# One step's opening of a filter block split in two: seeds copied a step ahead, factors and first products ahead of the slots

## The chip, the cores and the metric

The kernel runs on one core of one Trainium2 chip. The metric is the device time of one execution in microseconds (us). Engines: PE (TensorE, matrix products), DVE (VectorE), ACT (ScalarE), POOL (GpSimd) and SP (SyncE, which issues the DMAs). [...]

## What is computed

Two independent heads over 2048 positions and 448 channels, side by side in the output. Head A is a long convolution (S4D): its filter K is a sum over 256 complex states per channel, applied by FFT. Head B is softmax attention with 16 heads of 28 channels.

```
def _A_ref(u, log_A_real, A_imag, C_real, C_imag, log_dt, D_skip):
    dt = exp(log_dt); A = -exp(log_A_real) + 1j * A_imag
    C = (C_real + 1j * C_imag) * dt[:, None]
    P = exp((A * dt[:, None])[:, :, None] * pos[None, None, :])
    K = 2.0 * einsum("dn,dnl->dl", C, P).real
    y = irfft(rfft(u_t, 2 * L) * rfft(K, 2 * L), 2 * L)[:, :, :L]
    return y.transpose(0, 2, 1) + u * D_skip
def _B_ref(x, wqkv, wo):
    q, k, v = split(x @ wqkv)               # 16 heads of 28
    p = softmax(q @ k.T * scale)
    return (p @ v) @ wo
return concatenate([a, b], axis=-1)
```

## The kernel before

The kernel has three parts in time. Up to about 260 us it projects q, k and v and makes the seeds of the filter (functions inside the first `with`). Then a loop of NS = 256 steps does the attention; into its gaps goes everything else of head A. A short tail ends it.

A step is one block of 128 keys for one block of 512 queries and four heads. Its order is written out by hand in `ORDER` (line 33), and every engine keeps the order of the program in this part (`KEPT["a"]`). The entries of `ORDER`:

- `m0` to `m3` (`max_mm`, line 166): one score product per head for the row maximum of a later step, written into a buffer `pm` of PSUM. `m0` (shown as `pm<-kdif,qhat`) is read by ACT (`rl`, Relu), `m1` by a custom DVE instruction that also reads `rl`, `m2` and `m3` by a DVE maximum (`mx<-pm`).
- `s0` to `s3` (`s_mm`, line 700): the scores of this step into one of three buffers `pss`; ACT makes the exponential `p` from each.
- `pv` (`pv_step`, line 707): the product of the previous step's `p` with v, `po<-p,v`.
- `f`: a slot (`slot`, line 936), a place for one other piece of work that uses PE. `slot` takes, in this order, urgent work (sums, scaling and maxima of a finished block of queries), output projections, the products of a filter block (`m_due`), the transform of u (`u_due`), and spectrum and finish jobs of the convolution. A slot with nothing due stays empty. Its product also goes to a buffer `pm`.
- `v` (`vec`, line 975): takes one operation from the queue of DVE work of the open filter block.
- `k`: closes a finished filter block (`k_next`, line 968), opens one where it is due (`k_begin`, line 951), and issues three of its POOL operations.

`pm` has three buffers taken in turn by `w_tile` (line 123), until the filter blocks are done; then a ring of four.

A filter block is the filter of eight channels; there are NB = 56, and block b is due at step 3.5 b. It has two tables, e (built on POOL by nine operations, `e_power`, line 620) and g (built on DVE by nine queue entries, `g_powers`, line 634). Both grow by doubling from seeds that a DMA has brought as `sdb` (three buffers, `load_sd`). g also needs the factors `zg`, a bank of PSUM of its own with one buffer. The first entry of g's queue, `lowest`, is three small operations on 128x128 elements; the others are one operation each (`first(1, 8)`, `second(1, 8)` and its addition on 128x256; `first(2, 16)` on 128x512; two halves of `second(2, 16)` and their additions on 128x256). With three `v` and three POOL operations a step, a block is built in three steps.

`k_start` (line 609) opens a block: it takes buffers for e, g and zg and makes three copies on ACT: the seeds of g, the factors zg, the seeds of e. It is called by `k_begin`, which then fills the queues and sets the products of the block due KD = 5 steps later: two tasks of 16 products on e and g (`k_mm`, `pm<-e,g`), evicted by ACT as `ko`, then one on `ko` (`pm<-w,ko`), evicted as `yk`. e and g have two buffers each, so a block's seeds overwrite those of the block before last; `done["mm"]` keeps which block's products are issued.

From step 192 on, spectrum jobs fill the slots (`spectrum`, line 762): two forward tasks (`pm<-yk,mw`, whose DVE products are `pr`, and `p` on DVE and POOL behind the second) and two backward ones (`pm<-p,mw`), and then finish jobs.

Of the kernel before, what the change touches and what calls it, by code (L numbers as in the profile page):

```python
# [7 lines left out]
F32 = mybir.dt.float32  # L8
F32R = mybir.dt.float32r
I32 = mybir.dt.int32  # L10
AF = mybir.ActivationFunctionType
# [12 lines left out]
CQ = 512  # L24
# [5 lines left out]
NU = G * NQ  # L30
NS = NU * NK
LEAD = 3
ORDER = ('m0', 's0', 'm1', 's1', 'v', 'f', 'pv', 'k', 'f', 'v', 'm2', 's2', 'm3', 's3', 'v')
PB = 8
F1 = 2
FX, PD, GAP = 1, 2, 2
# [5 lines left out]
K0, KP, KD, UP = 0, 3.5, 5, 3  # L42
# [14 lines left out]
SDF = F_Z + 18 * 16  # L57
Z_G = 9 * 16
# [30 lines left out]
def body(ctx, tc, a, out):  # L89
    nc = Engines(tc)  # L90
# [4 lines left out]
    def pool(stack, name, bufs=1, space=None, side=None):  # L95
        kw = {} if space is None else {"space": space}
        if side:
            kw["side"] = side
        return stack.enter_context(tc.tile_pool(name=name, bufs=bufs, reuse_waits="tile", **kw))
# [450 lines left out]
    ps_g = pool(ps_st, "ps_g", 1, PSUM)  # L550
# [52 lines left out]
    sds, egs = {}, {}  # L603

    def load_sd(b):
        sds[b] = g_p.tile([128, SDF], F32, name="sdb", bufs=3)
        nc.sync.dma_start(sds[b], sd_d[b // BO][b % BO])

    def k_start(b):
        sd = sds[b]  # L610
        e = g_p.tile([128, 2, 16, N2], F32, name="e", bufs=2)
        g = g_p.tile([128, 2, 16, N1], F32, name="g", bufs=2)
        zg = ps_g.tile([128, CQ], F32, name="zg")
        egs[b] = e, g
        zgs[b] = zg
        nc.scalar.activation(g[:, :, :, :4], sd[:, F_G:F_Z].rearrange("p (c h e) -> p c h e", c=2, e=4), AF.Copy)
        nc.scalar.activation(zg[:, :Z_G], sd[:, SDF - Z_G:], AF.Copy)
        nc.scalar.activation(e[:, :, :, :8], sd[:, :F_G].rearrange("p (c h e) -> p c h e", c=2, e=8), AF.Copy)

    def e_power(b, i, q):  # L620

        t, m = egs[b][0], 8 << i
        zz = sds[b][:, F_Z:].rearrange("p (k f h) -> p k f h", k=6, f=3)
        if q == 0:
            zr = zz[:, i, 0, :][:, None, :, None].to_broadcast([128, 2, 16, m])
            nc.gpsimd.tensor_tensor(t[:, :, :, m:2 * m], t[:, :, :, :m], zr, ALU.mult)
        elif q == 1:
            uts[0] = g_p.tile([128, 2, 16, 32], F32, name="eu")[:, :, :, :m]
            zi = zz[:, i, 1:3, :][:, :, :, None].to_broadcast([128, 2, 16, m])
            nc.gpsimd.tensor_tensor(uts[0], t[:, ::-1, :, :m], zi, ALU.mult)  # L630
        else:
            nc.gpsimd.tensor_tensor(t[:, :, :, m:2 * m], t[:, :, :, m:2 * m], uts[0], ALU.add)

    def g_powers(b):

        t, zg = egs[b][1], zgs[b]
        zz = zg[:, :Z_G].rearrange("p (k f h) -> p k f h", k=3, f=3)
        tt = nc.vector.tensor_tensor

        def first(i, m):  # L640
            tt(t[:, :, :, m:2 * m], t[:, :, :, :m], zz[:, i, 0, :][:, None, :, None].to_broadcast([128, 2, 16, m]), ALU.mult)

        def second(i, m, c):
            n = c.stop - c.start
            u = zg[:, CQ // 2:CQ // 2 + n * 16 * m].rearrange("p (c h m) -> p c h m", c=n, m=m)
            zi = zz[:, i, 1 + c.start:1 + c.stop, :][:, :, :, None].to_broadcast([128, n, 16, m])
            tt(u, t[:, ::-1, :, :m][:, c], zi, ALU.mult)
            return lambda: tt(t[:, c, :, m:2 * m], t[:, c, :, m:2 * m], u, ALU.add)
        both, u = slice(0, 2), {}

        def lowest():
            first(0, 4)
            second(0, 4, both)()
        ops = [lowest, lambda: first(1, 8), lambda: u.update(a=second(1, 8, both)), lambda: u["a"](), lambda: first(2, 16)]
        for c in (slice(0, 1), slice(1, 2)):
            ops += [lambda c=c: u.update(a=second(2, 16, c)), lambda: u["a"]()]
        return ops

    uts, zgs = {}, {}
# [56 lines left out]
    def load_og(u):  # L716
        og_u[u] = og = kq_p.tile([128, G - 1, CQ], F32, name="og")
        nc.sync.dma_start(og, on_d[u % NQ][:G - 1].rearrange("g p q -> p g q"))
# [138 lines left out]
    powers = {"g": collections.deque(), "e": collections.deque()}  # L857
    done = {"mm": -1}
# [19 lines left out]
    k_due = collections.deque(range(NB))  # L878
# [31 lines left out]
    def f_slot(s_, kind):  # L910
        f_load(s_, kind)
        if not f_tasks[kind]:
            if not f_loaded[kind] or f_loaded[kind][0][0] > s_:
                return False
            f_tasks[kind].extend(f_loaded[kind].popleft()[1])
            f_load(s_, kind)
        gap, t = f_tasks[kind][0]
        if n_slot[0] < f_next[kind] + gap:
            return False
        f_tasks[kind].popleft()  # L920
        t()
        s_done[0] += kind == "s" and not f_tasks[kind]
        f_next[kind] = n_slot[0]
        f_load(s_, kind)
        return True
# [10 lines left out]
    def slot(s_):  # L936
# [11 lines left out]
        else:  # L948
            f_slot(s_, "s") or f_slot(s_, "f")

    def k_begin(s_):
        if not (k_due and K0 + k_due[0] * KP <= s_ and done["mm"] >= k_due[0] - 2 and not powers["e"] and not powers["g"]):
            return
        b = k_due.popleft()
        k_start(b)
        powers["g"] += g_powers(b)
        powers["e"] += [lambda i=i, q=q: e_power(b, i, q) for i in range(3) for q in range(3)]
        p0, p1, p2 = k_mm(b)

        def m1():  # L960
            p1()
            done["mm"] = b
        m_due.extend((s_ + KD, t_) for t_ in (p0, m1, p2))
        last[0] = b
# [3 lines left out]
    def k_next():  # L968

        if last[0] is not None and not powers["e"] and not powers["g"]:  # L970
            if last[0] + 2 < NB:
                load_sd(last[0] + 2)
            last[0] = None

    def vec():
        if powers["g"]:
            powers["g"].popleft()()

    prev = None
    for s in range(NS):  # L980
        u, kt = divmod(s, NK)
        sm = s + NK + LEAD
        if s == 12 * NK:
            k0_st.close()
            f_p["s", 0] = f_p["s", 1] = pool(f0_st, "f0_p", side="right")
            f_ready["s", 0], f_ready["s", 1] = s, NS
        if s >= 12 * NK and f_ready["s", 1] == NS and not (k_due or m_due or powers["g"] or powers["e"]):
            g_st.close()
            ps_st.close()
            ps_w[:] = pool(ps_st, "ps_f", 4, PSUM), 1  # L990
            f_ready["s", 1] = s + F1
        if kt == 12 and u // NQ == G - 1:
            load_og(u)
        late[0] = s + NK + LEAD > NS
        if u % NQ == NQ - 1 and u < NU - 1 and kt % 4 == 2:
            load_v(u // NQ + 1, kt // 4)
        if sm < NS and sm // NK % NQ == NQ - 1 and sm % NK % 4 == 0 and sm % NK and sm // (NQ * NK) + 1 < G:
            load_kd(sm // (NQ * NK) + 1, sm % NK // 4 - 1)
        if sm < NS and sm % (NQ * NK) == 0 and sm:
            load_kd(sm // (NQ * NK), HG - 1)  # L1000
        if kt % 4 == 1 and u % NQ == 1 and u // NQ + 1 < G:
            load_k(u // NQ + 1, kt // 4, k_pools[(u // NQ + 1) % 2])
        if kt == 2:
            if u + 2 < NU:
                load_q(u + 2)
        ps = []
        for op in ORDER:
            if op[0] == "s":
                ps.append(s_mm(u, kt, int(op[1])))
            elif op[0] == "f":  # L1010
                slot(s)
            elif op[0] == "v":
                vec()
            elif op == "k":
                k_next()
                k_begin(s)
                for _ in range(3):
                    if powers["e"]:
                        powers["e"].popleft()()
            elif op == "pv":  # L1020
                if prev:
                    pv_step(*prev)
                    if prev[1] == NK - 1:
                        fin(prev[0], s)
            elif sm < NS:
                max_mm(sm // NK, sm % NK, int(op[1]))
        for _ in range(FX if late[0] else 0):
            slot(s)
        if sm < NS and sm % NK == NK - 1:
            def end(un=sm // NK):  # L1030
                max_end(un, w_tile())
                max_put(un)
            max_join(sm // NK)
            soon_slot(UG[0], end)
        k_next()
        prev = (u, kt, ps)
    pv_step(*prev)
    fin(prev[0], NS)
    s = NS
# [63 lines left out]
```

## Time and profile before

| | us |
|---|---|
| median of 3 runs | 1368.82 |
| lowest and highest | 1365.33, 1370.16 |
| the profiled execution's own time | 1366.65 |
| its span, first to last instruction | 1364.9 |
| PE busy in the span | 1243.5 |
| DVE busy | 980.3 |
| ACT busy | 968.6 |
| POOL busy | 831.0 |
| mean granted clock of TensorE | 0.975 of full speed |

All instructions of the loop show line 73, that of a helper, so groups are told apart by the names of what they write and read: `g<-g,zg` is an operation on table g, `e<-e,eu` one on e, `mx<-pm` a row maximum, `po<-p,v` PV. In a timeline the columns are start, duration (of the merged row), engine, line, operation, written and read tiles with shapes, count, and in brackets the idle time of the engine before it with what ended it. Rows of matrix products overlap: the modelled end of one lies behind the start of the next, so their spacing is read from the starts. In a list of waits the columns are the total, the number and the longest.

### The profile page before, as it was taken

To read this page: it belongs to the slowest core of one execution; us is meant where nothing else is said; L and a number is where in the kernel's file an instruction comes from. 1 tells how busy PE (TensorE), PEld (TensorE's weight loads), DVE (VectorE), ACT (ScalarE), POOL (GpSimd) and SP (SyncE) were. 2 spreads that over 40 slices of the span, in tenths; PEclk is the share of its full clock that TensorE was granted. 3 is DMA by queue.
4 is the path that set the end of the run, shared out by engine and by line. 5 is a ranking of instruction groups with operands and counts; after the bars stand their busy time and mean duration, and the time that the engine had idled before them with its cause. 6 is when DMAs were issued, how large, how long until landed. Compare 5 with 4: busy or idle time off the path is not lost.

```text
span 1364.9 us, 33230 instructions
## 1 busy us (share of the span) xinstructions
PE 1243.5 (91%) x12625; PEld 707.2 (52%) x12625; DVE 980.3 (72%) x2138; ACT 968.6 (71%) x2069; POOL 831.0 (61%) x705
## 2 busy tenths in 40 slices
PE   6978784799999999999999999999998999998997
PEld 4866662355555555555555555555555545544433
DVE  5778765877777777777788888887887766857311
ACT  4867662488888888888888888878786665655553
POOL 3576661187877877878878988888896111202221
PEclk9988896999999999999999999999999999999999
DMA  6775679726675546378533233632324544636476
GB/s 194 241 243 193 219 263 246 208 62 140 160 168 119 131 125 155 109 205 209 161 96 88 64 72 78 148 86 66 77 66 139 181 123 154 208 109 205 138 192 178
DMA packets 200729, 205.37 MB, mean 150 GB/s; under 512 B 96632, under 2 KB 159160, under 8 KB 198520
## 3 DMA queue, kind: packets, MB, share of 16 engines
q1 hardware_dynamic: 200568, 203.23, 53.5%
q8 instruction: 100, 1.64, 0.5%
q14 instruction: 61, 0.50, 0.1%
HBM read 120.73 MB, written 82.18 MB: 149 GB/s over the span
## 4 chain that ended last, share of the span: by engine, by line
PE 58%; DVE 16%; ACT 11%; POOL 5%; DMA 5%; issue 3%; SPq 0%; ACTq 0%; DVEq 0%; POOLq 0%
PE pm L73 34%; PE po L73 13%; PE pss L73 12%; ACT p L73 6%; DVE mx L73 3%; POOL qhat L73 3%; DVE g L73 2%; ACT rl L73 2%; DVE p L73 2%; DMA khat<-k 2%; DVE tri L73 1%; DVE pr L73 1%; DVE px L73 1%; POOL x_e L73 1%; DVE sg L73 1%
## 5 line engine op out<-in xcount | busy, mean ns | idle before, releaser
L73 ACT ACTIVATE p<-pss 128x512 f32<-128x512 f32 x1024 | 565.3, 608 | 137.0 <-PE pss L73 128.4
L73 PE MATMUL pss<-qhat,khat 128*128 128x512 f32 x1024 | 402.2, 399 | 3.5 <-ACT p L73 3.4
L73 DVE TENSOR_REDUCE mx<-pm 128x1 f32<-128x512 f32 x500 | 321.4, 683 | 104.6 <-PE pm L73 103.4
L73 PE MATMUL pm<-khat,qhat 128*128 128x512 f32 x749 | 329.7, 443 | 41.5 <-DVE mx L73 36.1
L73 POOL TENSOR_TENSOR e<-e,sdb 128x256 f32<-128x256 f32 x168 | 201.9, 1202 | 166.0 <-ACT e L73 157.0
L73 PE MATMUL po<-p,v 128*32 128x512 f32 x2048 | 271.8, 598 | 0.0
L73 POOL TENSOR_TENSOR e<-e,eu 128x256 f32<-128x256 f32 x168 | 248.5, 1479 | 13.2
L73 PEld LDWEIGHTS pm<-khat,qhat 128*128 128x128 f32 x749 | 141.0, 189 | 217.7 <-DVE mx L73 83.4
L73 PEld LDWEIGHTS pss<-qhat,khat 128*128 128x128 f32 x1024 | 190.6, 188 | 45.9 <-issue 11.1
L73 DVE CUSTOM_DVE_ANT_0 rl<-pm,rl 128x512 f32<-128x512 f32 x249 | 171.5, 689 | 47.3 <-ACT rl L73 44.2
L73 POOL TENSOR_TENSOR eu<-e,sdb 128x256 f32<-128x256 f32 x168 | 201.8, 1201 | 0.0
L73 DVE TENSOR_TENSOR g<-g,zg 128x128 f32<-128x128 f32 x392 | 162.9, 416 | 46.6 <-ACT zg L73 41.5
L73 ACT ACTIVATE rl<-pm 128x512 f32<-128x512 f32 x249 | 150.8, 606 | 24.9 <-PE pm L73 24.9
L73 POOL TENSOR_TENSOR p<-pr,pr 64x448 f32<-64x448 f32 x32 | 40.9, 1277 | 191.7 <-DVE pr L73 180.6
L73 PE MATMUL pm<-kdif,qhat 128*128 128x512 f32 x249 | 100.9, 405 | 2.4 <-DMA v<-v 1.3
L73 PEld LDWEIGHTS pm<-e,g 128*32 128x32 f32 x3584 | 63.0, 110 | 52.8 <-issue 30.9
L73 DVE TENSOR_TENSOR zg<-g,zg 128x128 f32<-128x128 f32 x224 | 87.5, 391 | 1.9
L73 PEld LDWEIGHTS po<-p,v 128*32 128x32 f32 x2048 | 56.5, 110 | 42.6 <-issue 37.9
L73 PE MATMUL pm<-e,g 128*32 128x64 f32 x3584 | 72.5, 220 | 0.0
L73 ACT ACTIVATE y<-pm 128x448 f32<-128x448 f32 x48 | 26.3, 548 | 63.5 <-PE pm L73 30.9
L73 PE MATMUL pm<-xh,wh 112*128 112x512 f32 x128 | 56.2, 443 | 11.2 <-DVE tl L73 5.1
L73 DVE TENSOR_TENSOR pr<-pm,ub 128x448 f32<-128x448 f32 x64 | 37.0, 619 | 32.7 <-PE pm L73 32.7
(137 smaller groups left out, 1555.4 us busy)
## 6 DMA issues: line engine op xcount, KB each, us to landing
sdb<-sd SPq DMA_DIRECT2D x56, 336.0 KB
qhat<-q SPq DMA_DIRECT2D x64, 256.0 KB
khat<-k SPq DMA_DIRECT2D x64, 256.0 KB
sd<-sg SPq DMA_DIRECT2D x8, 1456.0 KB
mw<-in_mw SPq DMA_DIRECT2D x16, 512.0 KB
sd<-qhat SPq DMA_DIRECT2D x8, 896.0 KB
yk<-yk SPq DMA_DIRECT2D x56, 128.0 KB
yu_d<-ub SPq DMA_DIRECT2D x64, 112.0 KB
```

The lines of the kernel that those rows point to most:

```text
L73: i = f(*args, **kw)
```

## The change

The opening is split. `k_seeds` takes the buffers of e and g and makes their two copies on ACT. It is called from `k`, behind PV, by `k_seed`, one step before the block is due, once the products of the block before last are issued. `k_start` keeps the buffer of zg and its copy, and is called by `k_begin` from a new entry `b` of `ORDER`, right behind `s1`, ahead of the step's first `v`. `k_begin` now asks that the block has its seeds, instead of asking for the products of the block before last. `k_next` is called in `b` too.

```
-ORDER = ('m0', 's0', 'm1', 's1', 'v', 'f', 'pv', 'k', 'f', 'v', 'm2', 's2', 'm3', 's3', 'v')
+ORDER = ('m0', 's0', 'm1', 's1', 'b', 'v', 'f', 'pv', 'k', 'f', 'v', 'm2', 's2', 'm3', 's3', 'v')
...
-    def k_start(b):
+    def k_seeds(b):
         sd = sds[b]
         e = g_p.tile([128, 2, 16, N2], F32, name="e", bufs=2)
         g = g_p.tile([128, 2, 16, N1], F32, name="g", bufs=2)
-        zg = ps_g.tile([128, CQ], F32, name="zg")
         egs[b] = e, g
-        zgs[b] = zg
         nc.scalar.activation(g[:, :, :, :4], sd[:, F_G:F_Z].rearrange("p (c h e) -> p c h e", c=2, e=4), AF.Copy)
-        nc.scalar.activation(zg[:, :Z_G], sd[:, SDF - Z_G:], AF.Copy)
         nc.scalar.activation(e[:, :, :, :8], sd[:, :F_G].rearrange("p (c h e) -> p c h e", c=2, e=8), AF.Copy)
+
+    def k_start(b):
+        zgs[b] = ps_g.tile([128, CQ], F32, name="zg")
+        nc.scalar.activation(zgs[b][:, :Z_G], sds[b][:, SDF - Z_G:], AF.Copy)
...
+    def k_seed(s_):
+        if k_due and k_due[0] not in egs and K0 + k_due[0] * KP <= s_ + 1 and done["mm"] >= k_due[0] - 2:
+            k_seeds(k_due[0])
+
     def k_begin(s_):
-        if not (k_due and K0 + k_due[0] * KP <= s_ and done["mm"] >= k_due[0] - 2 and not powers["e"] and not powers["g"]):
+        if not (k_due and K0 + k_due[0] * KP <= s_ and k_due[0] in egs and not powers["e"] and not powers["g"]):
             return
         b = k_due.popleft()
         k_start(b)
...
+            elif op == "b":
+                k_next()
+                k_begin(s)
             elif op == "k":
                 k_next()
-                k_begin(s)
+                k_seed(s)
                 for _ in range(3):
                     if powers["e"]:
                         powers["e"].popleft()()
```

In a step that opens a block DVE's queue had: the custom maximum of m1, (the last operation of the block before), `lowest`, the maxima of m2 and m3, `first(1, 8)`. It now has: the custom maximum of m1, `lowest`, `first(1, 8)`, the maxima of m2 and m3, `second(1, 8)`. ACT's queue had the three copies behind PV, after the eviction of the step's first slot; it now has the copy of zg behind the exponential of s1, and the two other copies stand behind PV of the step before.

## The prediction

> **What bounds the kernel now.** I read the page first, for the span and the engines' shares, then the stage windows. The change touches only the 56 filter blocks, which run beside the attention steps from 266 us to about 1043 us.
>
> ```profile
> span 1364.9 us, 33230 instructions
> ```
> ```profile
> 266.00:698.00 432.00, 421.17 (x4899) 229.72 (x4899) 330.01 (x780) 357.50 (x810) 346.03 (x272) 1.00 0.58 144
> 698.00:1015.00 317.00, 298.99 (x3576) 171.14 (x3576) 260.90 (x620) 257.23 (x568) 273.43 (x216) 1.00 0.35 82
> ```
>
> The columns are length, then busy time of PE, PEld, DVE, ACT and POOL, then the granted clock. PE fills 97% of the first stretch (blocks plus the transforms of u) and 94% of the second (blocks alone). So PE sets the time, and only what makes it wait counts. The waits of PE alone, by stretch (698 to 1015 first, then 266 to 698):
>
> ```profile
> PE pm L73 <- DVE mx L73: 18.0, 26, 1.3
> ```
> ```profile
> PE pm L73 <- DVE mx L73: 10.5, 21, 1.5
> ```
>
> It waits for one thing, the row maximum on DVE (`mx`) that frees a buffer of the three-buffer ring `pm`: 28.5 us in 47 waits, and there are 56 blocks. The timeline shows that these waits follow the opening of a block. This is a step without slots (a slot is one of the two places `f` for other work on PE), by engine: ACT, then DVE, then PE.
>
> ```profile
> 814.97 0.71 ACT L73 ACTIVATE yk<-pm 128x256 f32<-128x256 f32 x1
> 816.06 1.09 ACT L73 ACTIVATE p<-pss 128x512 f32<-128x512 f32 x2 [0.38 <-PE pss L73]
> 817.03 0.60 ACT L73 ACTIVATE rl<-pm 128x512 f32<-128x512 f32 x1
> 817.51 1.10 ACT L73 ACTIVATE p<-pss 128x512 f32<-128x512 f32 x2
> 818.46 0.34 ACT L73 ACTIVATE g<-sdb 128x128 f32<-128x128 f32 x1
> 818.66 0.33 ACT L73 ACTIVATE zg<-sdb 128x144 f32<-128x144 f32 x1
> 818.88 0.45 ACT L73 ACTIVATE e<-sdb 128x256 f32<-128x256 f32 x1
> ```
> ```profile
> 819.02 0.29 DVE L73 TENSOR_TENSOR g<-g,zg 128x128 f32<-128x128 f32 x1 [0.66 <-ACT zg L73]
> ```
> ```profile
> 819.88 1.28 DVE L73 TENSOR_REDUCE mx<-pm 128x1 f32<-128x512 f32 x2
> ```
> ```profile
> 819.53 0.40 PE L73 MATMUL pss<-qhat,khat 128*128 128x512 f32 x1
> 820.62 0.50 PE L73 MATMUL pm<-khat,qhat 128*128 128x512 f32 x1 [0.69 <-DVE mx L73]
> ```
>
> ACT copies g, zg and e in a row after the two exponentials `p`. DVE stands 0.66 us at the first operation on g until zg lands, spends 0.86 us (819.02 to 819.88) on its three `lowest` operations, and only then takes the maximum of m2. PE's m1 of the next step needs that maximum's buffer: it comes 1.09 us after s0, where rows of PE otherwise follow each other in 0.23 us (809.06 to 809.30 in the fence below). So such a begin costs 0.86 us.
>
> **The change, part by part.** *The zg copy, alone, right behind s1.* In the step above it would start where the g copy starts, 818.46 for 818.66: `lowest` begins 0.20 us earlier. *The first operations one `v` earlier.* `lowest` now fills the `v` ahead of the slots, so `first(1, 8)`, which stood behind both maxima, moves up to the `v` ahead of m2 and into the way of the maximum. The next rows are DVE and PE after another begin without slots, where the next step has none either.
>
> ```profile
> 805.40 1.28 DVE L73 TENSOR_REDUCE mx<-pm 128x1 f32<-128x512 f32 x2
> 806.60 0.41 DVE L73 TENSOR_TENSOR g<-g,zg 128x256 f32<-128x256 f32 x1
> 806.93 0.68 DVE L73 CUSTOM_DVE_ANT_0 rl<-pm,rl 128x512 f32<-128x512 f32 x1
> 807.54 0.08 DVE L73 DVE_READ_ACCUMULATOR2_ANT mx<- 128x1 f32 x1
> 807.54 0.42 DVE L73 TENSOR_TENSOR zg<-g,zg 128x256 f32<-128x256 f32 x1
> 808.00 0.42 DVE L73 TENSOR_TENSOR g<-g,zg 128x256 f32<-128x256 f32 x1
> 808.34 1.29 DVE L73 TENSOR_REDUCE mx<-pm 128x1 f32<-128x512 f32 x2
> 809.54 0.68 DVE L73 TENSOR_TENSOR g<-g,zg 128x512 f32<-128x512 f32 x1
> ```
> ```profile
> 809.06 0.40 PE L73 MATMUL pss<-qhat,khat 128*128 128x512 f32 x1
> 809.30 0.40 PE L73 MATMUL pm<-khat,qhat 128*128 128x512 f32 x1
> ```
>
> `first(1, 8)` takes 0.33 us of DVE (806.60 to 806.93). Gain 0.20, loss 0.33: the maximum of m2, and with it PE's m1, comes 0.13 us later. Behind it the order is shifted too: the 0.68 us operation (809.54) stands ahead of the next maximum where a 0.42 us one stood (808.00), and one with a spacing of 0.46 (807.54 to 808.00) replaces one of 0.33 ahead of `rl`. That maximum moves by 0.13 + 0.13 + about 0.2, from 808.34 to about 808.8; the first half of 1.28 us then ends near 809.5, where PE, itself 0.13 late, asks for it at 809.43. So 0.1 us more, in the half of the blocks whose next step has no slot; with a slot PE arrives later and it is nothing.
>
> *The copies of g and e, one step ahead behind PV.* That step holds the third product of an older block, with its eviction yk. ACT is done with it at 815.68 and waits until 816.06 for PE. The g copy takes 0.20 us of ACT (818.46 to 818.66), the e copy at most its 0.45: they fill the 0.38 us and push the exponentials by 0 to 0.27 us. I take 0.05, since two neighbouring ACT rows overlap (818.66 and 818.88 are 0.22 apart at 0.33 long). ACT then runs without a break from 816.06 to the copies, so this goes into zg. Without that idle time it would cost 0.65.
>
> *A begin with one slot.* ACT, DVE and PE, in that order:
>
> ```profile
> 424.57 1.11 ACT L73 ACTIVATE p<-pss 128x512 f32<-128x512 f32 x2
> 425.52 0.59 ACT L73 ACTIVATE ub<-pm 128x448 f32<-128x448 f32 x1
> ```
> ```profile
> 426.52 0.29 DVE L73 TENSOR_TENSOR g<-g,zg 128x128 f32<-128x128 f32 x1 [1.09 <-ACT zg L73]
> ```
> ```profile
> 427.38 0.68 DVE L73 TENSOR_REDUCE mx<-pm 128x1 f32<-128x512 f32 x1
> ```
> ```profile
> 427.35 0.39 PE L73 MATMUL pss<-qhat,khat 128*128 128x512 f32 x1
> 428.12 0.50 PE L73 MATMUL pm<-khat,qhat 128*128 128x512 f32 x1 [0.38 <-DVE mx L73]
> ```
>
> Here the copies wait for the slot's eviction ub; PE loses 0.77 - 0.23 = 0.54 us. After, zg starts at ub's place, 425.52, and lands with the 0.36 that lay between zg and `lowest` above (818.66 to 819.02): 425.88 for 426.52, 0.64 earlier. Less 0.33 for `first(1, 8)`, PE gains 0.31 and still loses 0.23. *With two slots* the maximum follows its own product, so nothing is lost or won:
>
> ```profile
> 612.43 0.50 PE L73 MATMUL pm<-khat,qhat 128*128 128x512 f32 x1
> ```
> ```profile
> 613.02 0.68 DVE L73 TENSOR_REDUCE mx<-pm 128x1 f32<-128x512 f32 x1
> ```
>
> *Conditions.* In the built order the blocks begin at steps 0, 4, 7 ... 193 before and 1, 4, 8, 11 ... 196 after: seeds need the products of the block before last one step sooner, so a block that an urgent task delays can no longer catch up, and the last one comes three steps later. The step count and the final slots stay the same. Around step 196 the first spectrum job now has its second task in a begin step, and the second job's falls on step 200, while the ring still has three buffers. What one such task did before (DVE, then PE):
>
> ```profile
> 1047.51 2.67 DVE L73 TENSOR_TENSOR p<-pr,pr 64x448 f32<-64x448 f32 x2
> 1050.10 0.68 DVE L73 TENSOR_REDUCE mx<-pm 128x1 f32<-128x512 f32 x1
> ```
> ```profile
> 1050.84 0.70 PE L73 MATMUL pm<-khat,qhat 128*128 128x512 f32 x1 [2.51 <-DVE mx L73]
> ```
>
> One wait of 2.5 us before; after, two tasks with one step's slot work each instead of two in one step. Bounds: both as long, +2.5, or each half, 0, and below it -1 if POOL's part is earlier out of the way. I take +2 as the second stands in the same ring. [...]
>
> *POOL.* It stood idle for the e copy:
>
> ```profile
> POOL e L73 <- ACT e L73: 157.0, 44, 49.9
> ```
>
> This wait shrinks and is worth nothing, since the PE waits above name DVE alone. The loads of sdb are issued at the end of a step instead of behind the next PV, half a step earlier, and are needed one step earlier; none of the waits above is for them.
>
> **The sum.** Second stretch: 26 begins, all but a few without slots: 26 x (0.13 + 0.05) + 13 x 0.1 = +6.0. First stretch: before 11 begins with one slot and 4 without, 11 x 0.54 + 4 x 0.86 = 9.4 (10.5 in the PE row); after 16 and 3, 16 x 0.23 + 3 x 1.04 = 6.8; so -2.6. Spectrum +2. Together +5.4 on the profiled execution's 1366.65 us (span 1364.9): 1372. The median of the runs shown, 1368.82, lies 2.2 above that execution; by it the sum is 1374. I forecast 1372, slower by 0.4%. A measurement of this kernel tells about 0.3%, 4.1 us, from no change.
>
> **The rivals.** *Faster: the earlier zg decides.* If `first(1, 8)` hides because DVE stands idle ahead of the maximum anyway, only the gains are left: 16 x 0.54 and 29 x 0.20 make -14.4, so 1352. For it: DVE's 1.09 us wait with one slot. Against: without slots the maximum starts right behind `lowest` (819.88), so there is no idle time to hide in. It decides wherever DVE waits over 0.33 us between `lowest` and m2's product. *No change.* Half of the second stretch's cost is taken up by the slots in the next steps, and the spectrum's by POOL: 3.0 - 2.6 + 0, so 1367. For it: PE's waits there are 0.69 us on average, against 0.86 of PE loss in the begin that I worked out. *Slower by more.* DVE is at 82% of the second stretch; if the delay is not absorbed in the next step, a begin costs the whole 0.46 by which the next maximum moves, and 0.1 twice: 26 x 0.66 = 17.2, less 2.6, makes 1381. Against: in the rows above DVE reaches `rl` of the step after next without a queue. That the change does not do what it says is excluded by the built order: the copies stand a step ahead and zg behind s1.
>
> **How the numbers follow.** The forecast gets 0.42, no change 0.30, faster 0.16, slower by more 0.12. The forecast's own range is 1367 to 1377; 0.08 of its chance lies under 4.1 us, and 0.02 of no change below -4.1. So faster 0.16 + 0.02 = 0.18; the same 0.28 + 0.08 = 0.36; slower 0.34 + 0.12 = 0.46. The unknown costs end at 26 x (-0.20) - 16 x 0.54 - 1 = -15 and at +15; the range 1361 to 1381 leaves out the faster rival's far half and the end of the slow one.
>
> **What would show it.** Right: in the second stretch the DVE row g<-ACT zg shrinks, yet PE's wait for mx grows from 18.0 to 21 us or more; in the first stretch it falls from 10.5 to about 8; four operations on g stand in a row ahead of the maximum, which starts later behind s1 than the 2.4 us from 817.51 to 819.88. Wrong: PE's wait in the second stretch falls, which would mean that `first(1, 8)` is hidden or zg lands earlier than one copy; or the time changes outside 266 to 1068 us.

## The result and the profile after

The changed kernel takes 1377.87 us (median of six runs, 1373.09 to 1381.67), the kernel before 1367.64 us beside it (six runs, 1365.33 to 1370.16). The ratio is 1.0073, 95% interval 1.0047 to 1.0099: slower by some 10 us, where 5.4 were forecast. Another six runs (e8 below) gave 1374.26 us against 1366.53, ratio 1.0067, 95% interval 1.0042 to 1.0092. The forecast of 5.4 lies just below both intervals, which begin at 6.4 and 5.7 us. The profiled execution is the slowest of its six, 1381.67 us, and a part of its 15 us is its own, as the stages show below.

The page of the changed kernel begins with the span; the two lines from the windows have the columns of the prediction (length, then busy time of PE, PEld, DVE, ACT and POOL, then the granted clock).

```profile
span 1379.9 us, 33243 instructions
```
```profile
266.00:698.00 432.00, 419.64 (x4806) 227.76 (x4806) 327.71 (x771) 352.19 (x803) 341.97 (x270) 1.00 0.55 142
698.00:1015.00 317.00, 296.94 (x3513) 167.75 (x3515) 256.33 (x607) 252.25 (x559) 263.96 (x208) 1.00 0.34 83
```

In the second of these stretches 328 rows of PE write `pss`, where 334 did before; a step has four. So the same 317 us hold one and a half steps less work in the slower kernel, and its waits come out too small. These are the waits of the changed kernel by the prediction's stretches, 698 to 1015 us first:

```profile
PE pm L73 <- DVE mx L73: 19.6, 28, 1.0
```
```profile
PE pm L73 <- DVE mx L73: 8.7, 26, 1.0
```

18.0 us became 19.6 and 10.5 became 8.7: together no change at all. So I cut by work instead. A step is four matmuls that write `pss`; where those rows start gives the same steps in every run. Steps 100 to 192 are the blocks with few other slots. The windows and PE's waits in them, before and after:

```profile
675.60:1026.60 351.00, 331.86 (x3960) 189.57 (x3959) 288.60 (x686) 285.35 (x634) 302.14 (x238) 1.00 0.35 86
```
```profile
PE pm L73 <- DVE mx L73: 19.1, 28, 1.3
```
```profile
678.50:1035.80 357.30, 334.90 (x3903) 188.58 (x3902) 288.76 (x683) 284.24 (x633) 299.27 (x236) 1.00 0.34 82
```
```profile
PE pm L73 <- DVE mx L73: 22.0, 31, 1.0
```

Now the same steps take 6.3 us longer. Their slots differ a little: 8 products of the transform of u more and 64 on e and g less, 0.9 us of PE against 1.0, which about cancels. PE's wait for the maximum grows by 2.9 us and its busy time by 3.0; a part of the latter is the same stall, since a product that follows a wait is recorded at 0.50 us instead of 0.39 (rows below). The whole span, cut this way (us; the first step begins at the first column's time):

| run | loop begins | steps 0-100 | 100-192 | 192-209 | 209 to end | span |
|---|---|---|---|---|---|---|
| before | 262.3 | 413.3 | 351.0 | 77.7 | 260.6 | 1364.9 |
| after | 263.0 | 415.5 | 357.3 | 83.4 | 260.7 | 1379.9 |
| after, second profile (e8) | 261.1 | 412.0 | 357.3 | 82.4 | 260.6 | 1373.5 |
| e1 | 260.2 | 407.2 | 347.2 | 78.1 | 259.2 | 1351.9 |
| e2 | 260.9 | 428.8 | 365.3 | 78.2 | 258.9 | 1392.1 |
| e3 | 259.3 | 410.1 | 352.1 | 82.6 | 260.8 | 1364.9 |
| e5 | 262.4 | 411.9 | 357.2 | 71.7 | 272.3 | 1375.5 |
| e6 | 260.5 | 425.3 | 362.2 | 81.4 | 260.5 | 1389.9 |
| e7 | 263.0 | 400.7 | 344.7 | 81.5 | 260.5 | 1350.4 |
| e9 | 260.7 | 413.2 | 348.3 | 83.2 | 260.9 | 1366.3 |
| e10 | 262.9 | 401.3 | 331.0 | 76.7 | 260.6 | 1332.5 |
| e11 | 262.4 | 402.7 | 332.2 | 80.0 | 260.3 | 1337.5 |
| e12 | 264.3 | 411.1 | 341.3 | 80.1 | 260.6 | 1357.3 |

The start of the loop differs by 5 us between profiles whose program is the same up to there, so single profiles are compared by stage. Before to after: 6.3 us in steps 100 to 192, 5.7 (4.7 in the second profile of the changed kernel) around the spectrum in steps 192 to 209, nothing behind step 209. Steps 0 to 100 hold a pause of 2.6 us that the second profile does not have (its step takes 7.38 us instead of 4.17); without it they are 1 us shorter.

A begin without slots after the change, ACT and DVE and PE in order of time:

```profile
816.29 1.11 ACT L73 ACTIVATE p<-pss 128x512 f32<-128x512 f32 x2
...
817.24 0.34 ACT L73 ACTIVATE zg<-sdb 128x144 f32<-128x144 f32 x1
...
817.62 0.29 DVE L73 TENSOR_TENSOR g<-g,zg 128x128 f32<-128x128 f32 x1 [0.47 <-ACT zg L73]
...
817.94 0.30 DVE L73 TENSOR_TENSOR zg<-g,zg 128x128 f32<-128x128 f32 x1
...
818.27 0.74 DVE L73 TENSOR_TENSOR g<-g,zg 128x128 f32<-128x128 f32 x2
818.31 0.40 PE L73 MATMUL pss<-qhat,khat 128*128 128x512 f32 x1
...
818.93 1.28 DVE L73 TENSOR_REDUCE mx<-pm 128x1 f32<-128x512 f32 x2
...
819.67 0.50 PE L73 MATMUL pm<-khat,qhat 128*128 128x512 f32 x1 [0.96 <-DVE mx L73]
820.00 0.40 PE L73 MATMUL pss<-qhat,khat 128*128 128x512 f32 x1
```

The order is as foreseen: `zg` right behind the exponentials of s0 and s1, then four operations on g in a row (the x2 is the last of `lowest` with `first(1, 8)`), then the maximum. Against PE's s0 of the next step, `lowest` starts 0.69 us ahead of it (817.62 to 818.31), before 0.51 (819.02 to 819.53 in the prediction's rows): the earlier copy is worth 0.18. But from its start to the maximum lie now 1.31 us (817.62 to 818.93) and before 0.86. The one added operation costs 0.45, and m1 comes 1.36 us behind s0 instead of 1.09.

### The profile page after: what moved, and what is told of

It is laid out like the page before. It is cut to its first block, busy times and chain, and to the rows that moved or that the text cites. A ratio compares the mean times of both kernels' runs of the same rounds, so it can differ in the third digit from the quotient of the medians.

```text
span 1379.9 us, 33243 instructions
## 1 busy us (share of the span) xinstructions
PE 1252.9 (91%) x12625; PEld 709.7 (51%) x12625; DVE 983.8 (71%) x2138; ACT 965.6 (70%) x2069; POOL 831.0 (60%) x705
## 3 DMA queue, kind: packets, MB, share of 16 engines
q8 instruction: 100, 1.64, 0.5%
## 4 chain that ended last, share of the span: by engine, by line
PE 50%; DVE 19%; ACT 17%; POOL 5%; issue 4%; DMA 4%; SPq 1%; ACTq 0%; DVEq 0%; POOLq 0%
PE pm L73 29%; PE po L73 11%; ACT p L73 10%; PE pss L73 9%; DVE mx L73 4%; DVE g L73 4%; ACT rl L73 3%; POOL qhat L73 3%; DVE p L73 2%; DVE pr L73 1%; DVE tri L73 1%; DMA kdif<-kd 1%; ACT yk L73 1%; DVE zg L73 1%; DVE px L73 1%
## 5 line engine op out<-in xcount | busy, mean ns | idle before, releaser
L73 PE MATMUL pm<-khat,qhat 128*128 128x512 f32 x749 | 333.1, 448 | 44.5 <-DVE mx L73 38.3
L73 PEld LDWEIGHTS pm<-e,g 128*32 128x32 f32 x3584 | 66.1, 112 | 54.4 <-issue 37.1
L73 ACT ACTIVATE ko<-pm 128x64 f32<-128x64 f32 x112 | 26.3, 235 | 50.0 <-PE pm L73 49.4
```

The lines of the kernel that those rows point to most:

```text
L73: i = f(*args, **kw)
```

## The experiments

All ratios are to the kernel before in runs on the same chip.

**e1: zg early, the order of DVE as it was.** In the changed kernel the begin goes behind the first vector place, so that `lowest` stays in the second place and `first(1, 8)` behind m3.

```diff
-ORDER = ('m0', 's0', 'm1', 's1', 'b', 'v', 'f', 'pv', 'k', 'f', 'v', 'm2', 's2', 'm3', 's3', 'v')
+ORDER = ('m0', 's0', 'm1', 's1', 'v', 'b', 'f', 'pv', 'k', 'f', 'v', 'm2', 's2', 'm3', 's3', 'v')
```

> The changed kernel with its opening moved behind the first v of the step: the seeds stay a step ahead and zg's copy stays ahead of the slots, but DVE's order is that of before (lowest behind the slots, first(1, 8) behind both maxima). Steps and slots are those of the changed kernel. Theory A (DVE's order: first(1, 8) ahead of the maximum costs more than the earlier zg gains): PE's wait for mx from 698 to 1015 us falls from the changed kernel's level to below 18 us, to about 14 (26 x 0.15 less than before), and from 266 to 698 us to about 4; total 10 to 16 us under the changed kernel, about 1364. Theory B (the last blocks come three steps later and meet the spectrum jobs while pm has three buffers): the total falls by little, the long steps 197 and 201 stay at 8 to 10 us. Theory C (the two seed copies a step ahead delay ACT): no change against the changed kernel, 1378.

Measured: 1356.85 us (1353.73 to 1363.09), ratio 0.9935 (0.9914 to 0.9955), 7 us better than the total expected. PE's waits of this kernel, 266 to 698 us, then 698 to 1015:

```profile
PE pm L73 <- DVE mx L73: 4.4, 10, 0.7
```
```profile
PE pm L73 <- DVE mx L73: 13.3, 27, 0.7
```

One swapped pair in the list turns a loss of 0.7% into a gain of 0.65%. The earlier `zg` is worth having; that DVE's operations moved one place up, with `first(1, 8)` ahead of the maximum, made the loss. Not all of the difference is that: of the 21.6 us between the span of the second profile of the changed kernel and this one, 14.9 lie in steps 0 to 192, and 4.3 in steps 192 to 209. There PE waits as long as in the changed kernel (3.11 and 2.14 us), but the clock stayed at 1.00 from 1036 to 1070 us, behind both waits, which I take for chance (last section). This profile is the fastest of its six executions.

**e2: only the suspected cost, on the kernel before.** `first(1, 8)` is made a part of `lowest`; nothing else of the change.

```diff
         def lowest():
             first(0, 4)
             second(0, 4, both)()
+            first(1, 8)
-        ops = [lowest, lambda: first(1, 8), lambda: u.update(a=second(1, 8, both)), lambda: u["a"](), lambda: first(2, 16)]
+        ops = [lowest, lambda: u.update(a=second(1, 8, both)), lambda: u["a"](), lambda: first(2, 16)]
```

> The kernel before with one difference: first(1, 8) is issued in the same v as lowest, so that it stands ahead of the maxima as in the changed kernel; copies, opening and spectrum are those of before. Theory A: each begin loses 0.33 us, and 0.1 to 0.2 more where the next step has no slot; 26 x 0.45 in the second stretch and about 15 x 0.33 in the first, so 10 to 16 us over before, about 1381. Theories B and C: no change, 1367 to 1369.

Measured: 1393.39 us (1389.38 to 1394.79), ratio 1.0186 (1.0167 to 1.0205). PE's waits, in the same two stretches:

```profile
PE pm L73 <- DVE mx L73: 19.9, 25, 1.9
```
```profile
PE pm L73 <- DVE mx L73: 26.9, 26, 1.6
```

26 us for 56 blocks, 0.47 us a block, with waits that grow from 28.5 to 46.8 us. An operation of 0.41 us recorded length does not hide and costs all of it, and more than the 0.33 that its row takes on DVE. The later operations of the block move up one place here too, as in the changed kernel, so the 0.47 is the price of the whole shift; two spells of half clock, about 3.4 us in all, are in it as well (last section). With that the loss is above the range that was expected.

**e3: only the later blocks, on the kernel before.** The first block is due at step 3 instead of 0.

```diff
-K0, KP, KD, UP = 0, 3.5, 5, 3
+K0, KP, KD, UP = 3, 3.5, 5, 3
```

> The kernel before with every block due three steps later (K0 = 3 for 0), so that the last opens at step 196 and the spectrum jobs meet the blocks as in the changed kernel; the opening and DVE's order are those of before. Theory B: steps 195 to 203 take about 6 us longer, with two steps of 8 to 10 us where before has one of 8.2; total about 1373. Theory A: unchanged, 1366 to 1369.

Measured: 1366.99 us (twelve runs), ratio 1.0002 (0.999 to 1.0014). In all it costs nothing, yet its steps 192 to 209 are 4.9 us longer, as in the changed kernel. Steps 0 to 100 are 3.2 shorter, and in this profile the loop begins 3.0 earlier, which hides that.

**e5: the spectrum behind the blocks.** In the changed kernel the spectrum jobs of the last unit are held back for 12 steps, so that they do not meet the last block.

```diff
-            f_ready["s", 0], f_ready["s", 1] = s, NS
+            f_ready["s", 0], f_ready["s", 1] = s + 12, NS
```

> The changed kernel with the spectrum jobs allowed from step 204 instead of 192, so that none meets a filter block. Theory B: steps 195 to 203 lose their two long steps, 8 us less there; some of the spectrum and finish tasks now come later and lengthen the end by 0.6 to 0.8 us each (seven finish tasks more behind the last step), so the total lies 2 to 5 us under the changed kernel, 1373 to 1376. Theory A alone: the long steps are gone too only if they were made by the opening; the end is longer by about 5, so 1380 or more.

Measured: 1379.51 us (1377.3 to 1381.89), ratio 1.0089 (1.0072 to 1.0107). Against the profile after, steps 192 to 209 are 11.7 us shorter and the part behind them is 11.6 longer: what is held back is paid at the end. The jobs take their own time with them, so this run does not show what the meeting costs; it shows that waiting gains nothing.

**e9: only the seeds ahead.** In the changed kernel the begin, and with it the copy of `zg`, goes back behind PV; the seeds stay one step ahead and the blocks late.

```diff
-ORDER = ('m0', 's0', 'm1', 's1', 'b', 'v', 'f', 'pv', 'k', 'f', 'v', 'm2', 's2', 'm3', 's3', 'v')
+ORDER = ('m0', 's0', 'm1', 's1', 'v', 'f', 'pv', 'b', 'k', 'f', 'v', 'm2', 's2', 'm3', 's3', 'v')
```

> The changed kernel with the opening moved behind PV, right ahead of k: of the change only the copies of the g and e seeds a step ahead remain; zg's copy and lowest stand where they stood before. Steps and slots are those of the changed kernel. Theory A (the loss is DVE's order alone, the copies ahead are a gain): zg no longer waits behind the g copy, 0.2 us earlier at begins whose zg bank is free, so PE's wait for mx from 698 to 1015 us is 13 to 16 us (18.0 before, 19.6 in the changed kernel), total 1358 to 1365. Theory C (copies on ACT a step ahead delay the exponentials, and that delay is the loss): 1370 or more. If it equals the run with the opening behind the first v (1357), the early zg is worth nothing once the seeds are out of its way.

Measured: 1368.33 us (twelve runs), ratio 1.0015 (1.0004 to 1.0026), between the ranges of both theories. Steps 100 to 192 are 2.7 us shorter than before, steps 192 to 209 are 5.5 longer. The change can now be taken apart: seeds ahead +2, `zg` ahead of the slots as well -11 (e1; a part of it by chance, as said there), the operations on g one place earlier +17 to +21 (the changed kernel, 1374 to 1378).

**e8: the changed kernel once more**, with the others on their chip.

> The changed kernel once more, beside the others on one chip: 1373 to 1382. Its profiled execution had one step of 7.4 us at step 81, where PE stood 2.6 us in the middle of PV with nothing to wait for; if that belongs to the kernel it comes again at step 81, if it is chance the step is 4.0 us and the profiled span some 3 us shorter.

Measured: 1374.26 us (1371.52 to 1383.2), ratio 1.0067 (1.0042 to 1.0092); its stages are the third row of the table.

**e6 and e7: where may an operation on g stand?** In the changed kernel the second vector place, which holds `first(1, 8)` in a begin and the later operations of the block in other steps, moves between the maxima of m2 and m3 (e6) or behind both (e7).

```diff
-ORDER = (..., 'k', 'f', 'v', 'm2', 's2', 'm3', 's3', 'v')
+ORDER = (..., 'k', 'f', 'm2', 's2', 'v', 'm3', 's3', 'v')
+ORDER = (..., 'k', 'f', 'm2', 's2', 'm3', 's3', 'v', 'v')
```

> The changed kernel with the second v of every step moved from ahead of m2 to between s2 and m3: lowest stays ahead of the slots, first(1, 8) stands behind the maximum of m2 and ahead of that of m3. Theory A: the maximum of m2 then starts 0.2 us earlier than before in a begin without slots and 0.6 in one with a slot, the maximum of m3 0.1 later; PE's wait for mx is 11 to 15 us in the second stretch and about 4 in the first; total 1354 to 1362. If the early lowest were the loss and not first(1, 8): no better than the changed kernel, 1375.

> The changed kernel with the second v moved behind m3, next to the third: both maxima come ahead of first(1, 8) and second(1, 8), at the price of 0.4 us ahead of the next step's custom maximum. Theory A: both maxima 0.2 us earlier than before at begins without slots; PE's wait for mx 8 to 13 us in the second stretch, 3 in the first; total 1350 to 1358, if the later custom maximum does not hold m2 or m3 of the next step; if it does, waits of PE appear right behind PV and the total is 1360 to 1370.

Measured: e6 1389.17 us (1388.06 to 1391.68), ratio 1.017 (1.0156 to 1.0183), a clear miss; e7 1348.04 us (1344.97 to 1352.13), ratio 0.9871 (0.9854 to 0.9888). The rows of e6 in a step with the products of e and g show what I had overlooked:

```profile
885.99 0.69 DVE L73 TENSOR_REDUCE mx<-pm 128x1 f32<-128x512 f32 x1
...
886.60 0.68 DVE L73 TENSOR_TENSOR g<-g,zg 128x512 f32<-128x512 f32 x1
...
887.19 0.68 DVE L73 TENSOR_REDUCE mx<-pm 128x1 f32<-128x512 f32 x1
...
888.02 0.65 PE L73 MATMUL pm<-e,g 128*32 128x64 f32 x32 [0.44 <-DVE mx L73]
```

The buffer of m3 is not free until the second maximum, and the next slot of PE wants it. The groups of e6 between 266 and 1015 us (count, busy time and mean, then PE's idle time before the group and what ended it) have waits that the kernel before did not have at all:

```profile
L73 PE MATMUL pm<-khat,qhat 128*128 128x512 f32 x546 | 237.9, 436 | 11.0 <-DVE mx L73 11.0
L73 PE MATMUL pm<-e,g 128*32 128x64 f32 x3232 | 66.0, 220 | 16.9 <-DVE mx L73 16.8
L73 PE MATMUL pm<-w,ko 128*32 128x128 f32 x800 | 32.7, 278 | 9.6 <-DVE mx L73 7.8
```

m1 waits less, as hoped (11.0 against 28.4), but the slots of these two groups wait 25 us instead. Neither maximum may have an operation ahead of it. In e7 the waits of m1 that are left come from `lowest`, which still stands in the place behind s1. These are e7's rows at the end of a begin without slots; the first two are the last of `lowest`:

```profile
851.09 0.29 DVE L73 TENSOR_TENSOR zg<-g,zg 128x128 f32<-128x128 f32 x1
...
851.42 0.29 DVE L73 TENSOR_TENSOR g<-g,zg 128x128 f32<-128x128 f32 x1
851.47 0.40 PE L73 MATMUL pss<-qhat,khat 128*128 128x512 f32 x1
851.62 1.28 DVE L73 TENSOR_REDUCE mx<-pm 128x1 f32<-128x512 f32 x2
852.36 0.49 PE L73 MATMUL pm<-khat,qhat 128*128 128x512 f32 x1 [0.49 <-DVE mx L73]
```

m1 follows s0 after 0.89 us where 0.23 is free: better than 1.36, not yet good.

**e10: the late place alone, on the kernel before.** Nothing of the split opening; in the list of before the second place moves behind m3.

```diff
-ORDER = ('m0', 's0', 'm1', 's1', 'v', 'f', 'pv', 'k', 'f', 'v', 'm2', 's2', 'm3', 's3', 'v')
+ORDER = ('m0', 's0', 'm1', 's1', 'v', 'f', 'pv', 'k', 'f', 'm2', 's2', 'm3', 's3', 'v', 'v')
```

> The kernel before with only its order list changed: the second vector place of a step moved from ahead of the maximum of m2 to behind that of m3, nothing of the opening split. Theory (what counts is how many operations on g stand ahead of the maxima that free the buffers of products; the split of the opening is beside the point): the lowest level leaves the place ahead of the maximum of m2, where PE waited 28.5 us for maxima between 266 and 1015 us; the version of the changed kernel with this order kept 12.8 us of such waits, so about 16 us go: 1345 to 1355 us. Rival (the split is what makes the late order pay, since without it the lowest level still waits for its factors behind the weights of PV and the chain of one operation a place runs a step late into the E products): 1360 to 1372 us, with new waits of the E products for g.

Measured: 1333.48 us (1332.51 to 1335.18), ratio 0.9756 (0.974 to 0.9772): the fastest of all, and better than the theory allowed. I had carried over the 12.8 us of waits of e7, but in the kernel before the begin comes behind PV, so `lowest` too goes behind m3. What is left of 28.5 us, between 266 and 1015 us, by groups:

```profile
L73 PE MATMUL pm<-khat,qhat 128*128 128x512 f32 x588 | 254.6, 433 | 0.5 <-DVE mx L73 0.2
```

A begin's `lowest` in e10, and the two maxima behind it:

```profile
801.39 0.28 DVE L73 TENSOR_TENSOR g<-g,zg 128x128 f32<-128x128 f32 x1
801.71 0.30 DVE L73 TENSOR_TENSOR zg<-g,zg 128x128 f32<-128x128 f32 x1
...
802.04 0.74 DVE L73 TENSOR_TENSOR g<-g,zg 128x128 f32<-128x128 f32 x2
...
802.70 0.68 DVE L73 CUSTOM_DVE_ANT_0 rl<-pm,rl 128x512 f32<-128x512 f32 x1
...
804.13 1.29 DVE L73 TENSOR_REDUCE mx<-pm 128x1 f32<-128x512 f32 x2 [0.41 <-PE pm L73]
```

`lowest` no longer stands still for `zg`, since two maxima, 1.29 us together, lie between the copy and its first use, and the maximum starts when its product is there. The wait for `zg` between 266 and 1015 us, before, after the change and in e10, shrinks to nearly nothing here without any split:

```profile
DVE g L73 <- ACT zg L73: 40.4, 49, 2.0
```
```profile
DVE g L73 <- ACT zg L73: 23.6, 53, 0.5
```
```profile
DVE g L73 <- ACT zg L73: 0.5, 1, 0.5
```

**e11: both.** The list of e1 with the second place behind m3.

```diff
+ORDER = ('m0', 's0', 'm1', 's1', 'v', 'b', 'f', 'pv', 'k', 'f', 'm2', 's2', 'm3', 's3', 'v', 'v')
```

> The changed kernel with the begin behind the first vector place, as in the version at 1357 us, and the second vector place behind m3, as in the version at 1348 us. Theory (both take operations from ahead of the maximum of m2, the same operations, so they do not add): 1343 to 1352 us, not measurably apart from 1348. Rival (they add, 20 us and 26 us off the changed kernel): 1330 us or less.

Measured: 1339.54 us (1334.38 to 1342.02), ratio 0.9796 (0.9772 to 0.9819), between the two theories. The gains of e1 and e7 overlap but are not the same: e1's list takes `lowest` out of the place behind s1, where e7 left it. Beside e10 it shows that the split opening, under an order in which no maximum waits, has nothing left to give, and its later blocks cost 3.3 us in steps 192 to 209.

**e12: all three places behind m3**, in the changed kernel.

```diff
+ORDER = ('m0', 's0', 'm1', 's1', 'b', 'f', 'pv', 'k', 'f', 'm2', 's2', 'm3', 's3', 'v', 'v', 'v')
```

> The changed kernel with all three vector places behind m3. Theory (an operation costs only where a maximum that PE waits for stands behind it; behind m3 come m0 and m1 of the next step, whose maxima are then late by three operations, 1.0 to 1.2 us, against slots that take their buffers): part of the gain is given back, 1350 to 1362 us. Rival (any place behind m3 is free, since a step of PE has 3.0 us until the slots want the buffers): 1335 to 1345 us.

Measured: 1354.08 us (1351.92 to 1359.12), ratio 0.9912 (0.9888 to 0.9936). As the theory had it, the room behind m3 is limited; PE waits again, between 266 and 1015 us:

```profile
PE pm L73 <- DVE mx L73: 9.3, 36, 0.4
```

## Why the prediction held, and which terms were off

The direction and the reason were right: `first(1, 8)` in the way of the maximum of m2 costs more than the earlier `zg` gains. e1 and e2 show it from both sides, with the operation taken away from a kernel that has the early copy, and put alone into one that has not. The faster rival (the operation hides because DVE stands idle) falls with e2, where it cost 0.47 us a block.

*The second stretch, +6.0.* Measured +6.3 over steps 100 to 192, in both profiles of the changed kernel. The gain of 0.20 for the copy was 0.18. The loss of 0.33 was 0.45 in the begin shown above. A begin whose next step has no slot, with the step after it, grew by 0.38 us (4.05 + 3.94 to 4.26 + 4.11), where 0.28 was forecast, and one whose next step has the products of e and g by 0.26 (4.93 to 5.19) instead of 0.18. So the term per begin was a quarter to a third too small, and by difference the begins with other work beside them did better than I had counted. That the two errors left 6.3 for 6.0 is luck. The test that I set for it, a PE wait of 21 us or more between 698 and 1015 us, failed by its own stretch (19.6). By equal work the wait grows by 2.9 us (19.1 to 22.0), about the 3 that the test asked for, but that cut was made after the result. The others hold: DVE's wait for `zg` fell from 13.5 to 10.1 us there, and the maximum starts later than 2.4 us behind the exponentials, 2.64 (816.29 to 818.93).

*The first stretch, -2.6.* PE's wait fell from 10.5 to 8.7 us, about 8 was forecast. In time it is -1.3 in the second profile, and in the first +2.2, of which the pause is at least 2.6. The sign was right and half of the size came.

*The spectrum, +2.* This is the term that was mis-sized: +5.7 and +4.7. What was forecast of it, two waits instead of one, came nearly to the number. Before, PE waited 2.51 and 0.79 us there, after 2.94 and 2.14, so +1.8. DVE's two `p` operations took 2.67 us as before (first profile, 1057.14 to 1059.81), and POOL took up e at 1059.41, when they were nearly over. Left out was what follows such a wait. The granted clock of TensorE is the third column from the end; these are the windows behind the waits in the kernel before, in the second profile of the changed kernel, and in the first:

```profile
1050.50:1054.20 3.70, 3.36 (x18) 1.20 (x22) 1.58 (x4) 0.60 (x1) 0.00 (x0) 0.56 0.00 0
```
```profile
1056.50:1060.20 3.70, 3.70 (x74) 2.28 (x67) 1.65 (x5) 0.96 (x3) 3.53 (x4) 0.55 0.02 4
...
1077.00:1080.80 3.80, 3.80 (x73) 2.18 (x73) 1.03 (x3) 0.82 (x2) 0.00 (x0) 0.55 0.02 4
```
```profile
1059.50:1066.70 7.20, 5.80 (x77) 3.48 (x78) 4.23 (x10) 1.04 (x3) 6.89 (x7) 0.53 0.01 2
...
1083.60:1087.20 3.60, 3.60 (x73) 2.24 (x72) 0.71 (x3) 0.82 (x2) 0.00 (x0) 0.53 0.02 5
```

Length times what is missing from a full clock is what PE loses: 3.7 x 0.44 = 1.6 us before, 3.7 x 0.45 + 3.8 x 0.45 = 3.4 in the second profile, 7.2 x 0.47 + 3.6 x 0.47 = 5.1 in the first. Of that about 0.5 is not lost, since the half clock began at 1059.91, 1 us before the wait ended. With the waits these estimates make 1.8 + 1.8 = 3.6 of 4.7, and 1.8 + 3.0 = 4.8 of 5.7; the rest stays open. The change made a second long wait, and behind its two waits of 2.94 and 2.14 us came spells of 3.41 or 6.83 us. e3 gets the same cost there from the later blocks alone, so it belongs to the later blocks that the earlier seeds bring, not to the early `zg`.

*What was costed at nothing.* The wait of POOL for the copy of e did not shrink but grew, from 154.2 to 168.8 us between 266 and 1015 us, and that is worth as little as foreseen, since PE waits for no result of POOL there. The copies of the seeds behind PV were put at 0.05 a begin; with the later blocks they cost 2 us in all (e9), and the loss lies around the spectrum. Up to the loop and behind step 209 nothing changed that runs of one kernel do not show too. But one sign of being wrong came up by its letter: of the two waits at the spectrum the second stands at 1072 us before, past the bound of 1068, and steps 201 to 208, which begin there at 1068.8 us, grew by 3.3 us. The prediction had counted that wait and drew the bound too tight.

What I did not see, though the rows stood in the prediction, is that `lowest` in the kernel before did the same harm as `first(1, 8)` now does. I priced that begin at 0.86 us and then argued only over shifts of 0.1 to 0.3 within it. Moving the place for operations on g behind m3 takes all of it away (e10).

## What to carry to other kernels

Where an engine keeps the order of the program, as in this loop, the first question for a small operation is which buffer-freeing instruction stands behind it in the queue, before how early its operands can be had: here the operations on g in the place ahead of the maximum of m2 went with 28 us of waits of PE, and two maxima later, where their operands were ready as well, with almost none. Compare waits over equal work, not over equal time. And a long wait of the matrix engine should be priced with the slow clock that may follow: here waits of 1.57 to 2.94 us had a spell of half clock behind them, though not all did (1.59 us in the changed kernel, 3.11 in e1).

## What the runs showed of the hardware that was not expected

**Half clock behind a wait.** Behind waits of 2.51, 2.14 and 2.94 us the granted clock fell to one half (0.50 from 1050.97 to 1054.38 us before, from 1059.91 to 1066.74 and from 1083.81 to 1087.22 after). A PV of eight matmuls that otherwise takes 1.06 us took 1.94 in such a spell of the changed kernel:

```profile
1060.90 0.79 PE L73 MATMUL pm<-khat,qhat 128*128 128x512 f32 x1 [2.94 <-DVE mx L73]
...
1062.90 1.94 PE L73 MATMUL po<-p,v 128*32 128x512 f32 x8
```

At these waits a spell lasted 3.41 us or 6.83, never a length between, which at half clock is 1.7 us of PE's work or twice that: in the changed kernel the wait of 2.94 us was followed by the short one in the second profile and by the long one in the first, and the later wait of 2.14 by the short one in each. In the profiles before, after, e3, e8 and e11 the starts of two spells lie a whole number of such lengths apart (before, 1050.97 and 1235.29 us, 54; after, 1059.91 and 1083.81 us, 7), so I cut the time by a grid of 3.41 us that runs through them. PE was not idle for the whole of a window ahead of a spell. These are the window ahead of the spell in the kernel before, then in e1 the two windows over which its wait of 3.11 us was spread; the second column is PE's busy time:

```profile
1047.56:1050.97 3.41, 0.84 (x3) 0.43 (x4) 3.40 (x4) 1.61 (x4) 2.06 (x2) 1.00 0.37 149
```
```profile
1038.62 0.50 PE L73 MATMUL pm<-khat,qhat 128*128 128x512 f32 x1 [3.11 <-DVE mx L73]
```
```profile
1033.93:1037.34 3.41, 1.58 (x6) 0.96 (x6) 3.31 (x4) 2.06 (x4) 3.26 (x3) 1.00 0.47 186
1037.34:1040.76 3.42, 2.14 (x51) 1.23 (x55) 3.34 (x9) 0.82 (x2) 3.26 (x5) 1.00 0.02 5
```

The wait of 2.51 us left PE 0.84 us of one window, and half clock followed; the longer one was split and did not bring it. Cut by this grid from the start of the loop, the profiles before and after have six windows at full clock in which PE was busy for less than 1.50 us (0.84 to 1.28), and all six were followed by half clock; of the windows at full clock with more none was, the three lowest having 1.65 to 1.83 us. Two windows at half clock, with 2.43 and 2.40 us (after, from 1059.91 and 1240.82 us), were followed by a second one. So in these profiles a spell went with the share of one window that a wait took, and waits of one length differed: 2.14 us had a spell behind it in the changed kernel and none in e1. From 266 to 1028 us, where no wait for a maximum is longer than 1.5 us, the clock is under 0.99 in no single microsecond, before or after; in e2, waits of 1.57 and 1.64 us there had a spell behind each.

**A pause behind a late load of instructions.** In step 81 of some profiles PE stands still in the middle of a PV, with no engine named as the cause, and DVE and ACT then wait for PE. In the first profile of the changed kernel:

```profile
600.54 0.62 PE L73 MATMUL po<-p,v 128*32 128x512 f32 x2 [2.59 <-issue]
```

The same row waits 2.1 us in e1, 1.5 in e6, 1.8 in e11, 2.6 in e12 and not at all in the kernel before, in e9 or in the second profile of the changed kernel, which is the same program. The DMA records of the traces hold loads of instructions, 16 KB each on the queue `q8 instruction`. In all five profiles with the pause one of them starts 1.2 to 2.1 us after the start of step 81, and PE goes on 1.3 to 1.5 us after its end (here the load takes 597.95 to 599.22 us, and PE goes on at 600.54). In the profiles of changed kernels without the pause (e5, e7, e8, e9) the load at this place starts 2.8 to 4.2 us before the step. My reading is that PE stood for its next instructions; no run took the load away, so this was not shown, and why the load was late stays open. The clock stayed at 1.00 behind the pause, which was split over two windows of the grid, with PE busy for 2.26 us (595.70 to 599.12) and 1.99 us (599.12 to 602.53).
